# Giving out a load ring's slots by the program, and loading one weight matrix with one DMA, in a cached-attention decode kernel

## The chip, the core and the metric

The kernel runs on one core of one Trainium2 chip. The metric is device microseconds of one execution (us). Three runs of the kernel before gave 2533.29, 2533.44 and 2534.53 us; their median is 2533.44 us. One more execution was taken with the hardware profiler on: 2534.51 us.

## The reference: one decoding step of attention, mixed with a small feed-forward net

```
q = (x @ wq) as 32 heads of 128;   K, V caches: 32 heads x 65536 positions x 128, bf16
s = q . K * 128**-0.5;  p = softmax(s);  o = p @ V;   a = o @ wo
b = (silu(x @ w_gate) * (x @ w_up)) @ w_down          (512 -> 1792 -> 512)
g = sigmoid(sum(x * gate_w));   out = g * a + (1 - g) * b
```

x is one row of 512 numbers. The two caches are 512 MB each, together 1073.7 MB; w_gate, w_up and w_down have 1.835 MB each, wq and wo 4.19 MB each. Every byte of the caches is used once.

## The kernel before

**Tiles and steps.** Each head's cache is cut into G = 4 tiles of 16384 positions, so there are N = 128 K tiles and 128 V tiles, each of 4 MB: 128 partitions with 128 positions of 128 bf16 values, 32 KB in one piece per partition. The loop at line 355 goes through steps (n, v): K tile n and V tile v are loaded and worked on in one step. v trails n by 4, later by up to 8 (LAG, lines 344 to 352), and the last steps have a V tile alone.

**K tile n** (`products`, line 230; `scores`, line 249): VectorE multiplies the tile in place with the head's query (L240) and folds the 128 products of a position to 16 by three additions (L244). TensorE adds the last 16 with an identity matrix into the score bank S_ps (L254, 16 matmuls). After the fourth tile of a head, at the next step, come the maximum, the exponentials (L266 to L279) and, later, the sum.

**V tile v** (`values`, line 296): 32 matmuls (L302) with the exponentials as weights into O_ps. In one step TensorE runs values(v) first and scores(n) after it. After a head's last V tile the head is copied and turned to a column (L315, L323), and heads 0 to 15 are projected at once (`project`, L335); wo for heads 16 to 31 is loaded at the very end (`load_wo_end`, line 157) and these 16 heads are projected last.

**The ring.** All big loads (wq, K tiles, w_gate with w_up, w_down, V tiles, the last half of wo) go into one pool of SLOTS = 5 slots of 32 KB per partition (line 58, `big`, line 69). The pool hands a new tile the slot that its users gave back first. SyncE (SP) issues every load in the order of the program, and an issue waits until its slot's last users are done. In the trace, V tile 2 is issued at 107.05 us, when values(0) has ended, and K tile 7 at 111.39 us, when scores(4) has ended. The completions of all DMAs are counted on eight semaphores in turn, and an issue also waits for the DMA eight before it: the ninth DMA, first part of w_down, is issued at 8.41 us, when the first, x, has landed.

**The order at the start, on SP:** wq, K tile 0 in two halves, K tile 1, w_gate, w_up, gate_w (gwT, line 149), parts 0 and 1 of w_down (line 150), K tile 2, parts 2 to 7 of w_down (line 359), K tile 3, wo's first group (line 361), K tile 4, V tile 0, K tile 5, V tile 1 and so on. x itself (xT, line 76) comes over ScalarE's queue. w_down is laid out over 64 partitions, 28 KB each, and cut into eight DMAs of 8 partitions:

```
137	    HP = P // 2
138	    GT = F // HP
139	    wd_sb = wd_t[:HP, : GT * D].rearrange("p (t n) -> p t n", t=GT)
144	            lo = (0, 1, 2, 3, 32, 33, 34, 35)[i]
145	            part = slice(lo, lo + 29, 4)
146	            nc.sync.dma_start(out=wd_sb[part], in_=wd_rows[part])
```

**The feed-forward net** stands beside the first steps: `feed_forward_in` (line 169) after the products of step 1, `feed_forward_mid` (line 189) in step 2, ahead of the products. The mid part makes the hidden vector hT on VectorE, moves it from 128 to 64 partitions (two matmuls, L202, and a copy, L206), runs 28 matmuls with w_down (L209) and the gate's matmul (L213). `feed_forward_out` (line 218), after the products of step 3, scales the result and starts the output's accumulation with it (L226, L227).

**The end.** V tile 126 comes in two parts, tile 127 in five, and wo's last half in five (lines 365 to 367).

Of the kernel before, what the change touches and what calls it, by code (L numbers as in the profile page):

```python
# [8 lines left out]
ACT = mybir.ActivationFunctionType  # L9
ALU = mybir.AluOpType  # L10
AXIS = mybir.AxisListType
P = 128
# [3 lines left out]
NB = 128  # L16
SLOTS = 5
# [8 lines left out]
def kernel(  # L26
# [14 lines left out]
    nc = tc.nc  # L41
    bf16 = mybir.dt.bfloat16
    f32 = mybir.dt.float32

    _, H, Sk, Dh = A_k_cache.shape
    D = A_x.shape[2]
    F = B_w_gate.shape[1]
    KT = D // P
    FT = F // P
    G = Sk // (NB * P)  # L50
    NBH = Sk // P
    N = H * G
# [2 lines left out]
    scale = float(Dh) ** -0.5  # L55

    consts = ctx.enter_context(tc.tile_pool(name="consts", bufs=1))
    ring = ctx.enter_context(tc.tile_pool(name="ring", bufs=SLOTS))
    small = ctx.enter_context(tc.tile_pool(name="small", bufs=2))
    ppool = ctx.enter_context(tc.tile_pool(name="ppool", bufs=3))  # L60
    wo_pool = ctx.enter_context(tc.tile_pool(name="wo_pool", bufs=2))
# [3 lines left out]
    psum_m = ctx.enter_context(tc.tile_pool(name="psum_m", bufs=2, space=bass.MemoryType.PSUM))  # L65

    ctx.enter_context(tc.manual_schedule())

    def big(name):
        return ring.tile([P, NB * Dh], bf16, name=name, tag="big")  # L70


    xT = consts.tile([P, KT], bf16, name="xT")
    gwT = consts.tile([P, KT], bf16, name="gwT")
    with nc.allow_non_contiguous_dma(reason="small"):
        nc.scalar.dma_start(out=xT, in_=A_x[0, 0, :].rearrange("(p t) -> p t", t=KT))
    wq_t = big("wq_t")
    wq_sb = wq_t[:, : KT * H * Dh].rearrange("p (t f) -> p t f", t=KT)
    nc.sync.dma_start(out=wq_sb, in_=A_wq.rearrange("(p t) f -> p t f", t=KT))

    ident_f = consts.tile([P, P], f32, name="ident_f")
    make_identity(nc, ident_f[:])
    ident_b = consts.tile([P, P], bf16, name="ident_b")
# [15 lines left out]

    K_tiles, V_tiles, S_tiles, P_tiles, O_tiles = {}, {}, {}, {}, {}  # L100

    def load(dst, cache, n, name, cuts=(0, NB)):
        h, g = divmod(n, G)
        t = big(name)
        view = t.rearrange("p (j d) -> p j d", d=Dh)
        src = cache[0, h, g * NB * P : (g + 1) * NB * P, :].rearrange("(p j) d -> p j d", j=NB)
        for a, b in zip(cuts[:-1], cuts[1:]):
            nc.sync.dma_start(out=view[:, a:b, :], in_=src[:, a:b, :])
        dst[n] = view

    load(K_tiles, A_k_cache, 0, "K_t", (0, NB // 2, NB))
    load(K_tiles, A_k_cache, 1, "K_t")

    def queries(g):
        qg_ps = psum_m.tile([P, QG * Dh], f32, name="qg_ps", tag="misc")
# [13 lines left out]
        queries(g)  # L129


    gu_t = big("gu_t")
    wgu_sb = gu_t[:, : 2 * KT * F].rearrange("p (w t f) -> p w t f", w=2, t=KT)
    nc.sync.dma_start(out=wgu_sb[:, 0], in_=B_w_gate.rearrange("(p t) f -> p t f", t=KT))
    nc.sync.dma_start(out=wgu_sb[:, 1], in_=B_w_up.rearrange("(p t) f -> p t f", t=KT))
    wd_t = big("wd_t")
    HP = P // 2
    GT = F // HP
    wd_sb = wd_t[:HP, : GT * D].rearrange("p (t n) -> p t n", t=GT)
    wd_rows = B_w_down.rearrange("(p t) n -> p t n", t=GT)  # L140

    def load_wd(*which):
        for i in which:
            lo = (0, 1, 2, 3, 32, 33, 34, 35)[i]
            part = slice(lo, lo + 29, 4)
            nc.sync.dma_start(out=wd_sb[part], in_=wd_rows[part])

    with nc.allow_non_contiguous_dma(reason="small"):
        nc.sync.dma_start(out=gwT, in_=gate_w.rearrange("(p t) -> p t", t=KT))
    load_wd(0, 1)  # L150
    WG = 4
    wo_tiles = {}

    WH = H // 2
    wo_end = []

    def load_wo_end(cuts):
        t = big("wo_t")[:, : (H - WH) * D].rearrange("p (h n) -> p h n", n=D)
        rows = A_wo[WH * P :, :].rearrange("(h p) n -> p h n", p=P)
        for a, b in zip(cuts[:-1], cuts[1:]):  # L160
            nc.sync.dma_start(out=t[:, a:b, :], in_=rows[:, a:b, :])
        wo_end.append(t)

    def load_wo(g):
        wo_tiles[g] = wo_pool.tile([P, WG, D], bf16, name="wo_sb")
        rows = A_wo[g * WG * P : (g + 1) * WG * P, :]
        nc.sync.dma_start(out=wo_tiles[g], in_=rows.rearrange("(h p) n -> p h n", p=P))
# [21 lines left out]
    def feed_forward_mid(gu_sb, eg):  # L189
        nc.vector.tensor_scalar_add(eg, eg, 1.0)  # L190
        nc.vector.reciprocal(eg, eg)
        hprod = consts.tile([P, FT], f32, name="hprod")
        nc.vector.tensor_tensor(out=hprod, in0=gu_sb[:, :FT], in1=eg, op=ALU.mult)
        hT = consts.tile([P, FT], bf16, name="hT")
        nc.vector.tensor_tensor(out=hT, in0=hprod, in1=gu_sb[:, FT:], op=ALU.mult)
        xg = consts.tile([P, KT], f32, name="xg")
        nc.vector.tensor_tensor(out=xg, in0=xT, in1=gwT, op=ALU.mult)
        xs = consts.tile([P, 1], f32, name="xs")
        nc.vector.tensor_reduce(out=xs, in_=xg, axis=AXIS.X, op=ALU.add)
        h_ps = psum_m.tile([HP, GT], f32, name="h_ps", tag="misc")  # L200
        for r in range(2):
            nc.tensor.matmul(  # L202
                h_ps[:, r * FT : (r + 1) * FT], lhsT=ident_b[:, r::2], rhs=hT, start=True, stop=True
            )
        h2 = consts.tile([HP, GT], bf16, name="h2")
        nc.scalar.activation(out=h2, in_=h_ps, func=ACT.Copy)  # L206
        b_ps = psum_m.tile([1, D], f32, name="b_ps", tag="misc")
        for t in range(GT):
            nc.tensor.matmul(  # L209
                b_ps, lhsT=h2[:, t : t + 1], rhs=wd_sb[:, t, :], start=(t == 0), stop=(t == GT - 1)  # L210
            )
        g_ps = psum_m.tile([P, 1], f32, name="g_ps", tag="misc")
        nc.tensor.matmul(g_ps, lhsT=ones_f, rhs=xs, start=True, stop=True)  # L213
        eg2 = consts.tile([P, 1], f32, name="eg2")
        nc.scalar.activation(out=eg2, in_=g_ps, func=ACT.Exp, scale=-1.0)
        return b_ps, eg2

    def feed_forward_out(b_ps, eg2):

        nc.vector.tensor_scalar_add(eg2, eg2, 1.0)  # L220
        nc.vector.reciprocal(gval, eg2)
        rest = consts.tile([1, 1], f32, name="rest")
        nc.vector.tensor_scalar(
            out=rest, in0=gval[0:1, :], scalar1=-1.0, scalar2=1.0, op0=ALU.mult, op1=ALU.add
        )
        nc.scalar.activation(out=b_sb, in_=b_ps, func=ACT.Copy, scale=rest)  # L226
        nc.tensor.matmul(a_ps, lhsT=ones_f[0:1, 0:1], rhs=b_sb, start=True, stop=False)  # L227
# [117 lines left out]
    v = 0  # L345
# [8 lines left out]
    ff = done = tot_ps = None  # L354
    for n, v in steps:
        if n is not None and n > 1:
            load(K_tiles, A_k_cache, n, "K_t")
        if n == 2:
            load_wd(2, 3, 4, 5, 6, 7)
        if n == 3:  # L360
            load_wo(0)
        if v is not None:
            if v % (WG * G) == 2 * G and v // (WG * G) + 1 < WH // WG:
                load_wo(v // (WG * G) + 1)
            load(V_tiles, A_v_cache, v, "V_t", (0, NB) if v < N - 2 else (0, 64, NB) if v < N - 1 else (0, 32, 64, 96, 112, NB))
            if v == N - 1:
                load_wo_end((0, 4, 8, 12, 14, 16))
        if n == 2:
            ff = feed_forward_mid(*ff)
        halves = (0, NB // 2)  # L370
        vector = iter(()) if n is None else products(n)
        if n == 0:
            vector = (i for a in halves for i in products(n, a, a + NB // 2))
        top_of = None
        if n is None:
            top_of = H - 1 if S_tiles else None
        elif n % G == 0 and n > 0:
            top_of = n // G - 1
            vector = (i for a in halves for i in products(n, a, a + NB // 2))
        if top_of is not None:  # L380
            next(vector, None)
            mT_ps = row_max(top_of)
            next(vector, None)
            exponentials(top_of, mT_ps)
        for _ in vector:
            pass
        if n == 1:
            ff = feed_forward_in()
        if n == 3:
            feed_forward_out(*ff)  # L390
        if tot_ps is not None:
            weight(*tot_ps)
            tot_ps = None
        if done is not None:
            head_column(done, head_copy(done))
        if v is not None:
            values(v)
        if top_of is not None:
            tot_ps = top_of, total(top_of)
        if n is not None:  # L400
            scores(n)
        if done is not None and done < WH:
            project(done)
        done = v // G if v is not None and v % G == G - 1 else None
# [40 lines left out]
```

## Time and profile before

| What | Value |
|---|---|
| median of three runs | 2533.44 us |
| the profiled execution | 2534.51 us |
| its span, first to last instruction | 2532.6 us |
| read from HBM | 1087.64 MB, 429 GB/s over the span |
| VectorE (DVE) busy | 2175.5 us, 86% |
| TensorE (PE) busy | 1742.4 us, 69% |
| ScalarE (ACT) busy | 75.9 us, 3% |
| DMA queue q1 (SP's loads) | 42674 packets, 1087.66 MB, 99.7% of 16 engines' time |
| DMA queue q8 (instructions) | 53 packets, 0.87 MB, 0.1% |

The page cuts the span into 40 slices of 63.3 us and gives the DMA engines' share and rate in each. A load is cut into packets that 16 DMA engines move side by side; for each load the trace also holds the moment at which each of the engines that took part had counted its share as landed. "Spread" is used below for the time from the first of these counts to the last.

### The profile page before, as it was taken

The numbers are of one execution on the slowest core, as the hardware profiler recorded it, in microseconds if no ns is written. First come the engines' busy times: TensorE is split into PE (matmuls) and PEld (weight loads), VectorE is DVE, ScalarE is ACT, GpSimd is POOL, SyncE is SP. The second block draws the span as 40 slices with busy tenths as digits, with TensorE's granted clock in tenths as the row PEclk, the third lists the DMA queues.
The fourth block names the chain that finished last, engine by engine and source line by source line (L and its number), as shares of the span: only waits on it lengthen the run. The fifth ranks groups of instructions, "written<-read, shape, count | busy, mean of one in ns | idle before, by whom it ended". The sixth has DMA issues, their size and how long they took to land.

```text
span 2532.6 us, 15260 instructions
## 1 busy us (share of the span) xinstructions
PE 1742.4 (69%) x6738; PEld 712.1 (28%) x6738; DVE 2175.5 (86%) x784; ACT 75.9 (3%) x207; POOL 0.7 (0%) x6
## 2 busy tenths in 40 slices
PE   4677666776677666676776677667666776677679
PEld 2222222222222222222222223222222232222223
DVE  7998888888888999998888888888888888888860
ACT  1000000000000000000000000000000000000000
POOL 0000000000000000000000000000000000000000
PEclk7677777777777676677777777777777777777779
DMA  9999999999999999999999999999999999999998
GB/s 415 433 433 430 433 433 433 432 430 435 432 432 434 431 433 432 432 433 433 432 434 433 432 434 433 432 432 434 432 431 434 433 430 434 434 431 433 434 432 339
DMA packets 42884, 1088.63 MB, mean 430 GB/s; under 512 B 4737, under 2 KB 8834, under 8 KB 9090
## 3 DMA queue, kind: packets, MB, share of 16 engines
q1 hardware_dynamic: 42674, 1087.66, 99.7%
q8 instruction: 53, 0.87, 0.1%
q14 instruction: 13, 0.11, 0.0%
q10 hardware_dynamic: 144, 0.00, 0.0%
HBM read 1087.64 MB, written 0.00 MB: 429 GB/s over the span
## 4 chain that ended last, share of the span: by engine, by line
DMA 68%; PE 22%; DVE 10%; issue 1%; ACT 0%; DVEq 0%; SPq 0%
DMA V_t<-in_A_v_cache_dram 61%; PE O_ps L302 20%; DMA K_t<-in_A_k_cache_dram 5%; DVE K_t L240 5%; DVE K_t L244 5%; PE S_ps L254 1%; DMA wo_t<-in_A_wo_dram 1%; DMA wq_t<-in_A_wq_dram 0%; PE qg_ps L117 0%; DVE m L266 0%; PE oh_ps L323 0%; PE a_ps L335 0%; PE a_ps L227 0%; ACT P_sb L279 0%; DVE top L275 0%
## 5 line engine op out<-in xcount | busy, mean ns | idle before, releaser
L302 PE MATMUL O_ps<-V_t,P_sb 128*4 128x512 bf16 x4096 | 1157.3, 453 | 496.8 <-DMA V_t<-in_A_v_cache_dram 494.3
L240 DVE TENSOR_TENSOR K_t<-K_t,q_bc 128x16384 bf16<-128x16384 bf16 (+1 forms) x160 | 1117.2, 6983 | 254.4 <-DMA K_t<-in_A_k_cache_dram 232.9
L244 DVE TENSOR_TENSOR K_t<-K_t 128x4096 bf16<-128x4096 bf16 (+3 forms) x480 | 1030.9, 2148 | 14.3
L302 PEld LDWEIGHTS <-P_sb 128*4 128x4 bf16 x4096 | 393.9, 97 | 1241.0 <-issue 897.5
L254 PE MATMUL S_ps<-K_t,ident_b 128*128 128x128 bf16 x2048 | 466.0, 394 | 107.0 <-DVE K_t L244 106.9
L254 PEld LDWEIGHTS <-ident_b 128*128 128x128 bf16 x2048 | 227.6, 115 | 330.0 <-issue 140.2
L323 PE MATMUL oh_ps<-ident_f,O_sb 4*128 4x1 f32 x256 | 57.9, 343 | 74.1 <-ACT O_sb L315 74.1
L323 PEld LDWEIGHTS oh_ps<-ident_f,O_sb 4*128 4x128 f32 x256 | 55.2, 314 | 83.7 <-ACT O_sb L315 78.9
L270 PE MATMUL mT_ps<-diag,ones_f 128*128 128x128 f32 x64 | 23.6, 468 | 79.8 <-ACT diag L268 79.8
L268 ACT ACTIVATE diag<-ident_f,m 128x128 f32<-128x128 f32 x32 | 12.8, 401 | 2099.3 <-DVE m L266 2099.3
L317 DVE COPY O_sb<-O_ps 4x256 f32<-4x256 f32 x1 | 0.4, 414 | 52.1 <-ACT O_sb L315 52.1
L270 PEld LDWEIGHTS mT_ps<-diag,ones_f 128*128 128x128 f32 x64 | 14.7, 285 | 95.6 <-ACT diag L268 95.6
L266 DVE TENSOR_REDUCE m<-S_ps 128x1 f32<-128x512 f32 x32 | 21.9, 683 | 7.4 <-PE S_ps L254 7.4
L315 ACT ACTIVATE O_sb<-O_ps 4x512 f32<-4x512 f32 (+1 forms) x32 | 18.1, 566 | 131.0 <-PE O_ps L302 131.0
L279 ACT ACTIVATE P_sb<-S_ps,bias 128x512 bf16<-128x512 f32 x32 | 22.0, 687 | 1.0
L117 PE MATMUL qg_ps<-wq_t,X_bc 128*128 128x512 bf16 x32 | 8.6, 436 | 13.2 <-DMA wq_t<-in_A_wq_dram 13.2
L293 DVE RECIPROCAL recip<-tot_ps 128x1 f32<-128x1 f32 x32 | 5.1, 160 | 12.2 <-PE tot_ps L288 12.2
L209 PE MATMUL b_ps<-wd_t,h 64*1 64x512 bf16 x28 | 12.1, 629 | 4.3 <-DMA K_t<-in_A_k_cache_dram 4.3
L288 PEld LDWEIGHTS tot_ps<-rowsum,ones_f 128*128 128x128 f32 x64 | 9.5, 188 | 14.0 <-issue 14.0
L288 PE MATMUL tot_ps<-rowsum,ones_f 128*128 128x1 f32 x64 | 12.2, 260 | 0.0
L330 ACT ACTIVATE oT<-oh_ps,rg 128x1 bf16<-128x1 f32 x32 | 8.4, 263 | 76.6 <-PE oh_ps L323 76.6
L227 PE MATMUL a_ps<-b_sb,ones_f 1*1 1x512 f32 x2 | 1.9, 1032 | 12.1 <-ACT b_sb L226 12.1
(42 smaller groups left out, 73.8 us busy)
## 6 DMA issues: line engine op xcount, KB each, us to landing
K_t<-in_A_k_cache_dram SPq DMA_DIRECT2D x127, 4096.0 KB, 35.3
V_t<-in_A_v_cache_dram SPq DMA_DIRECT2D x126, 4096.0 KB, 29.1
wq_t<-in_A_wq_dram SPq DMA_DIRECT2D x1, 4096.0 KB
K_t<-in_A_k_cache_dram SPq DMA_DIRECT2D x2, 2048.0 KB, 16.8
V_t<-in_A_v_cache_dram SPq DMA_DIRECT2D x2, 2048.0 KB
V_t<-in_A_v_cache_dram SPq DMA_DIRECT2D x3, 1024.0 KB, 29.4
wo_sb<-in_A_wo_dram SPq DMA_DIRECT2D x4, 512.0 KB, 17.3
gu_t<-in_B_w_gate_dram SPq DMA_DIRECT2D x1, 1792.0 KB
```

Source lines behind the costliest of these rows:

```text
L209: nc.tensor.matmul(b_ps, lhsT=h2[:, t : t + 1], rhs=wd_sb[:, t, :], start=(t == 0), stop=(t == GT - 1))
L240: yield nc.vector.tensor_tensor(out=K, in0=K, in1=q_rep, op=ALU.mult)
L244: yield nc.vector.tensor_tensor(out=K[:, :, 0:half], in0=K[:, :, 0:half], in1=K[:, :, half : 2 * half], op=ALU.add,)
L254: nc.tensor.matmul(S_tiles[h][:, g * NB : (g + 1) * NB], lhsT=ident_b, rhs=K_tiles[n][:, :, c], start=(c == 0), stop=(c == WIDTH - 1),)
L266: nc.vector.tensor_reduce(out=m, in_=S_tiles[h], axis=AXIS.X, op=ALU.max)
L268: nc.scalar.activation(out=diag, in_=ident_f, func=ACT.Copy, scale=m)
L270: nc.tensor.matmul(mT_ps, lhsT=ones_f, rhs=diag, start=True, stop=True)
L279: nc.scalar.activation(out=P_tiles[h], in_=S_tiles[h], func=ACT.Exp, bias=bias, scale=scale, accum_out=rowsum[:, h : h + 1],)
L288: nc.tensor.matmul(tot_ps, lhsT=ones_f, rhs=rowsum[:, h : h + 1], start=True, stop=True)
L302: nc.tensor.matmul(O_tiles[h], lhsT=P_tiles[h][:, g * NB + j : g * NB + j + 4], rhs=V_tiles[n][:, j : j + 4, :], start=(g == 0 and j == 0) ...
L315: nc.scalar.activation(out=O_sb[:, :cut], in_=O_ps[:, :cut], func=ACT.Copy)
L323: nc.tensor.matmul(oh_ps, lhsT=O_sb[:, c * Dh : (c + 1) * Dh], rhs=ident_f[0:4, c : c + 1], start=(c == 0), stop=(c == 3),)
```

## The change

The pool of five slots becomes one tile `ring` of five slots' length, and `big` hands out its parts in strict rotation, the slot of five loads before; what a load waits for then follows from the part that it overwrites. w_down goes back to 128 partitions of 14 KB and is loaded by one DMA in step 3, behind K tile 3. x and gate_w change queues: gate_w goes over ScalarE's, x over SP's behind wq. wo's first group moves from step 3 to step 6. The mid part loses L202, L206 and its 28 matmuls; `feed_forward_out` runs 14 matmuls with w_down and moves ahead of the products of step 3. V tile 125 is loaded in two halves.

```diff
-    ring = ctx.enter_context(tc.tile_pool(name="ring", bufs=SLOTS))
+    ring = consts.tile([P, SLOTS * UNIT], bf16, name="ring")
+    taken = []
+    def big():
+        u = len(taken) % SLOTS
+        taken.append(u)
+        return ring[:, u * UNIT : (u + 1) * UNIT]
...
-        nc.scalar.dma_start(out=xT, in_=A_x[0, 0, :].rearrange("(p t) -> p t", t=KT))
+        nc.scalar.dma_start(out=gwT, in_=gate_w.rearrange("(p t) -> p t", t=KT))
...
     nc.sync.dma_start(out=wq_sb, in_=A_wq.rearrange("(p t) f -> p t f", t=KT))
+        nc.sync.dma_start(out=xT, in_=A_x[0, 0, :].rearrange("(p t) -> p t", t=KT))
...
-        nc.sync.dma_start(out=gwT, in_=gate_w.rearrange("(p t) -> p t", t=KT))
-    load_wd(0, 1)
+    wd_sb = wd_t[:, : FT * D].rearrange("p (t n) -> p t n", t=FT)
...
-        h_ps = psum_m.tile([HP, GT], f32, name="h_ps", tag="misc")
-        for r in range(2):
-            nc.tensor.matmul(
-                h_ps[:, r * FT : (r + 1) * FT], lhsT=ident_b[:, r::2], rhs=hT, start=True, stop=True
-            )
-        h2 = consts.tile([HP, GT], bf16, name="h2")
-        nc.scalar.activation(out=h2, in_=h_ps, func=ACT.Copy)
...
-        for t in range(GT):
-            nc.tensor.matmul(
-                b_ps, lhsT=h2[:, t : t + 1], rhs=wd_sb[:, t, :], start=(t == 0), stop=(t == GT - 1)
-            )
...
+    def feed_forward_out(hT, eg2):
+        b_ps = psum_m.tile([1, D], f32, name="b_ps", tag="misc")
+        for ft in range(FT):
+            nc.tensor.matmul(
+                b_ps,
+                lhsT=hT[:, ft : ft + 1],
+                rhs=wd_sb[:, ft, :],
+                start=(ft == 0),
+                stop=(ft == FT - 1),
+            )
...
-        if n == 2:
-            load_wd(2, 3, 4, 5, 6, 7)
         if n == 3:
+            nc.sync.dma_start(out=wd_sb, in_=B_w_down.rearrange("(p t) n -> p t n", t=FT))
+        if n == 6:
             load_wo(0)
...
-            load(V_tiles, A_v_cache, v, "V_t", (0, NB) if v < N - 2 else (0, 64, NB) if v < N - 1 else (0, 32, 64, 96, 112, NB))
+            load(V_tiles, A_v_cache, v, (0, NB) if v < N - 3 else (0, 64, NB) if v < N - 1 else (0, 32, 64, 96, 112, NB))
...
         if n == 2:
             ff = feed_forward_mid(*ff)
+        if n == 3:
+            feed_forward_out(*ff)
```

More of the change, by code (lines that the diff above doesn't have):

```diff
@@ L67 @@
     ctx.enter_context(tc.manual_schedule())
-    def big(name):
-        return ring.tile([P, NB * Dh], bf16, name=name, tag="big")
+    UNIT = NB * Dh
+    ring = consts.tile([P, SLOTS * UNIT], bf16, name="ring")
[4 more added lines that the diff above has]
+        return ring[:, u * UNIT : (u + 1) * UNIT]
     xT = consts.tile([P, KT], bf16, name="xT")
@@ L75 @@
     with nc.allow_non_contiguous_dma(reason="small"):
-        nc.scalar.dma_start(out=xT, in_=A_x[0, 0, :].rearrange("(p t) -> p t", t=KT))
-    wq_t = big("wq_t")
+        nc.scalar.dma_start(out=gwT, in_=gate_w.rearrange("(p t) -> p t", t=KT))
+    wq_t = big()
     wq_sb = wq_t[:, : KT * H * Dh].rearrange("p (t f) -> p t f", t=KT)
     nc.sync.dma_start(out=wq_sb, in_=A_wq.rearrange("(p t) f -> p t f", t=KT))
+    with nc.allow_non_contiguous_dma(reason="small"):
+        nc.sync.dma_start(out=xT, in_=A_x[0, 0, :].rearrange("(p t) -> p t", t=KT))
     ident_f = consts.tile([P, P], f32, name="ident_f")
@@ L100, with load @@
     K_tiles, V_tiles, S_tiles, P_tiles, O_tiles = {}, {}, {}, {}, {}
-    def load(dst, cache, n, name, cuts=(0, NB)):
+    def load(dst, cache, n, cuts=(0, NB)):
         h, g = divmod(n, G)
-        t = big(name)
+        t = big()
         view = t.rearrange("p (j d) -> p j d", d=Dh)
@@ L109, in load @@
         dst[n] = view
-    load(K_tiles, A_k_cache, 0, "K_t", (0, NB // 2, NB))
-    load(K_tiles, A_k_cache, 1, "K_t")
+    load(K_tiles, A_k_cache, 0, (0, NB // 2, NB))
+    load(K_tiles, A_k_cache, 1)
     def queries(g):
@@ L129 @@
         queries(g)
-    gu_t = big("gu_t")
+    gu_t = big()
     wgu_sb = gu_t[:, : 2 * KT * F].rearrange("p (w t f) -> p w t f", w=2, t=KT)
@@ L135 @@
     nc.sync.dma_start(out=wgu_sb[:, 1], in_=B_w_up.rearrange("(p t) f -> p t f", t=KT))
[L136 to L148, printed above, removed]
-        nc.sync.dma_start(out=gwT, in_=gate_w.rearrange("(p t) -> p t", t=KT))
-    load_wd(0, 1)
+    wd_t = big()
+    wd_sb = wd_t[:, : FT * D].rearrange("p (t n) -> p t n", t=FT)
     WG = 4
@@ L157, in load_wo_end @@
     def load_wo_end(cuts):
-        t = big("wo_t")[:, : (H - WH) * D].rearrange("p (h n) -> p h n", n=D)
+        t = big()[:, : (H - WH) * D].rearrange("p (h n) -> p h n", n=D)
         rows = A_wo[WH * P :, :].rearrange("(h p) n -> p h n", p=P)
@@ L199, in feed_forward_mid @@
         nc.vector.tensor_reduce(out=xs, in_=xg, axis=AXIS.X, op=ALU.add)
-        h_ps = psum_m.tile([HP, GT], f32, name="h_ps", tag="misc")
-        for r in range(2):
-            nc.tensor.matmul(
-                h_ps[:, r * FT : (r + 1) * FT], lhsT=ident_b[:, r::2], rhs=hT, start=True, stop=True
-            )
-        h2 = consts.tile([HP, GT], bf16, name="h2")
-        nc.scalar.activation(out=h2, in_=h_ps, func=ACT.Copy)
-        b_ps = psum_m.tile([1, D], f32, name="b_ps", tag="misc")
-        for t in range(GT):
-            nc.tensor.matmul(
-                b_ps, lhsT=h2[:, t : t + 1], rhs=wd_sb[:, t, :], start=(t == 0), stop=(t == GT - 1)
-            )
         g_ps = psum_m.tile([P, 1], f32, name="g_ps", tag="misc")
@@ L215, in feed_forward_mid @@
         nc.scalar.activation(out=eg2, in_=g_ps, func=ACT.Exp, scale=-1.0)
-        return b_ps, eg2
-    def feed_forward_out(b_ps, eg2):
+        return hT, eg2
+    def feed_forward_out(hT, eg2):
[8 more added lines that the diff above has]
+            )
         nc.vector.tensor_scalar_add(eg2, eg2, 1.0)
@@ L356 @@
         if n is not None and n > 1:
-            load(K_tiles, A_k_cache, n, "K_t")
-        if n == 2:
-            load_wd(2, 3, 4, 5, 6, 7)
+            load(K_tiles, A_k_cache, n)
         if n == 3:
+            nc.sync.dma_start(out=wd_sb, in_=B_w_down.rearrange("(p t) n -> p t n", t=FT))
+        if n == 6:
             load_wo(0)
@@ L388 @@
             ff = feed_forward_in()
-        if n == 3:
-            feed_forward_out(*ff)
         if tot_ps is not None:
```

## The prediction

> **What bounds the kernel now.** I read the page's strips first, then the table of stages, the chain at the end, and last the landing counts of single loads. On the page:
>
> ```profile
> PE 1742.4 (69%) x6738; PEld 712.1 (28%) x6738; DVE 2175.5 (86%) x784; ACT 75.9 (3%) x207; POOL 0.7 (0%) x6
> ...
> DMA  9999999999999999999999999999999999999998
> ...
> q1 hardware_dynamic: 42674, 1087.66, 99.7%
> q8 instruction: 53, 0.87, 0.1%
> ...
> DMA 68%; PE 22%; DVE 10%; issue 1%; ACT 0%; DVEq 0%; SPq 0%
> ```
>
> No compute engine is full; the DMA engines are, in every slice but the last. Two answers of the table of stages (us, busy of each engine, clock, DMA share, GB/s), one of the middle, one of the end, show where they are not:
>
> ```profile
> 1000.00:1500.00 500.00, 347.82 (x1319) 141.50 (x1320) 453.64 (x163) 14.19 (x40) 0.00 (x0) 0.74 1.00 433
> ```
> ```profile
> 2505.00:2510.00 5.00, 5.00 (x25) 1.99 (x24) 0.00 (x0) 0.00 (x0) 0.00 (x0) 1.00 0.95 401
> 2510.00:2515.00 5.00, 5.00 (x25) 1.99 (x24) 0.00 (x0) 0.00 (x0) 0.00 (x0) 1.00 0.91 365
> 2515.00:2520.00 5.00, 5.00 (x25) 1.97 (x24) 0.00 (x0) 0.00 (x0) 0.00 (x0) 1.00 0.79 287
> 2520.00:2525.00 5.00, 5.00 (x24) 1.87 (x22) 0.00 (x0) 0.00 (x0) 0.00 (x0) 1.00 0.54 148
> ```
>
> The share fades over 20 us instead of falling at once: some of the 16 DMA engines are done early and others late. The chain's last pieces name who waits for the late ones:
>
> ```profile
> 2472.70 31.39 DMA V_t<-in_A_v_cache_dram
> ...
> 2504.16 20.87 DMA wo_t<-in_A_wo_dram
> 2525.03 0.04 issue
> 2525.07 1.02 PE a_ps L335 x4
> 2526.09 0.98 PE oh_ps L323 x8
> 2527.07 2.69 PE a_ps L335 x12
> ```
>
> So the end is set by the DMA engine that lands its share last, plus 7.5 us (2525.07 to 2532.6). The fifth part of wo lands at 2529.11 and its first matmul starts at 2529.16, so even these 7.5 us hang on that engine.
>
> The landing counts tell when it falls behind. Up to w_up the 16 engines count within 0.74 us. After w_down's parts they stand in two halves, and they stay so (us after the first count, sorted):
>
> ```
> K tile 3 (first 60.10):   0 0 0 .1 .3 .3 .4 .4 | 8.3 8.4 8.4 8.4 8.5 8.7 8.8 9.9
> V 127, last part (2507.04): 0 0 6.8 6.8 6.9 7.1 7.4 7.8 8.3 8.4 8.5 8.6 9.1 12.7 15.5 16.6
> ```
>
> Each part of w_down shows one count about 1.1 us after its issue and eight later ones, and has 8 packets of 28 KB: all eight parts used the same eight engines (call them A; the others B), 8.35 us of work that B did not have. The rest of the spread grows slowly, as instruction packets (q8, 53 of 16 KB, 0.93 us each) fall on some engines: by following the steps of the sorted counts, some six of B and two or three of A. An A engine with both, 8.35 + 8.25 us, is the late one at 16.6.
>
> **The change, part by part.**
>
> *w_down in one DMA of 128 partitions.* Its shape is that of w_gate and w_up (128 packets of 14336 B, 8 on each of 16 engines). Between w_gate's and w_up's counts lie 40.49 - 36.17 = 4.32 us. So each engine gets 4.32 us where A had 8.35 and B nothing. The late A engine comes to 16.6 - 8.35 + 4.32 = 12.6; the latest of B, at 8.5 now, to 8.5 + 4.32 = 12.8. The later of the two counts: the end moves from 16.6 to 12.8, **-3.8 us**. The range of this term: if the instruction packets lie otherwise, one step of a sorted count is 1.2 to 1.4 us, so -2.5 to -5.2.
>
> *V tile 125 in halves.* K tile 0 in halves took (22.24 - 17.36) x 2 = 9.76 us where tile 1 whole took 31.92 - 22.24 = 9.68: **+0.1 us** on every engine. In return TensorE, idle for 1.62 us before tile 125 and then busy for 20.88 us up to 2525.02, starts up to 1.62 us earlier. Without that it would nearly follow the DMA anyway; with it, the last four matmuls on V tile 127 wait for its last part (2523.67 before). Both ends of the chain, wo's first part and TensorE, then move with the late DMA engine, so I take nothing more.
>
> *x behind wq.* x lands with wq (13.2 instead of 8.4), the four copies X_bc (0.63 us together) then come ahead of the queries, which start at about 13.7 instead of 13.23. K tile 0's first half lands at 18.05 and the first query group took 2.5 us (13.23 to 15.73), so 16.2 is early enough: 0. K tile 2's issue moves from 21.86 to 22.4, with loads queued to 41: 0.
>
> *Feed-forward.* TensorE loses 2 + 28 matmuls and gains 14: 12.10 us / 28 = 0.432, so 6.0 us instead of 12.4. It is not on the path, and neither are the small VectorE operations, which move from behind step 3's products to ahead of them. But K tile 5 takes w_down's slot and now waits for the 14 matmuls behind scores(2): VectorE's chain comes 0.8 us earlier (K tile 2 no longer behind two parts of w_down), scores(2) ends near 73.6, the matmuls at 79.7 (72.48 before). Behind K5 on SP stand V1, K6 and all later loads. The DMA engines run dry when V tile 0 is in: its first count 80.83 + 4.32 - 1.36 (wo's first group now comes later) = 83.8. An issue took 1.2 us to its first packet at the start (0.74 to 1.95): 80.9, 2.9 us to spare. Cost 0; without the cover a microsecond for each microsecond late.
>
> *Strict rotation.* Within a step the pool gave the next V load the slot of values (two steps back), the next K load that of scores. Rotation gives V the slot of K tile n-2, free after scores(n-2), some 3.65 us later (16 matmuls L254), and K the older slot of a V tile, but behind V on SP. So V issues come about 3.7 us later, K issues about the same. A steady V load was issued some 29 us ahead of its last landing, of which its own 9.68 us is transfer; 25 us is left, 15 us of queue in front of it. The thinnest place is V tile 2: issued after scores(4), 110.6, first packet 111.8; K tile 6 and wo's group are in at 109.89 + 4.32 = 114.2. 2.4 us to spare: 0. The later waits of wo's parts are for landings of V parts, which come earlier with the late engine. Bounds for all these holds together: 0 and, with both thin places missed by as much as they have to spare, 5 us.
>
> *Fewer DMAs.* Seven landing packets less on each A engine, 9 ns each: in the 4.32 already.
>
> Sum: -3.8 + 0.1 = **-3.7 us**. On the profiled execution 2534.51 gives 2530.8; its median runs are 1.07 us below it, so 2533.44 gives **2529.7 us**, -0.15%. About 0.2% (5.1 us) is what a measurement of this kernel can tell from no change, so this counts as the same, on the fast side.
>
> **A rule against it.** A late engine only matters if each engine has a rate of its own. In the last slices, when three engines are left, an 8 KB packet takes 0.309 us, as with 16 at work; 32 KB packets take 1.213 us at the median and at the 99th percentile. The Trainium skill's page "DMA: Bandwidth & Descriptors" (Where 436 GB/s comes from) says that a transfer from HBM is bound on the HBM side, at about 358 GB/s per core; by that the bytes alone would count, sharing them out otherwise would give 0, and the time would stay at 2533.4. This trace disagrees: 433 GB/s for 500 us on end.
>
> **Rivals.**
> 1. *The spread is there, but evening it out gives nothing:* the shared rate binds, or the instruction packets fall on other engines, so that another one is as late as now. For it: where those packets fall is read off sorted counts, not seen. Against: the packet times above and the halves after w_down. 0 + 0.1 gives 2533.5. Chance 0.14.
> 2. *More than counted:* the late engine has one instruction packet less (1.2 to 1.4 us) and TensorE's earlier start helps the last heads: -3.7 - 1.3 - 0.4 gives 2528.0, just past -0.2%. Chance 0.10.
> 3. *Slower: w_down's slot is given back late.* If the 14 matmuls run behind scores(3) instead of ahead of it (86.6 + 3.65 = 90.3, then 6.0: 96.3), K tile 5's first packet comes at 97.5, 13.7 us after the queue is empty: 2529.7 + 13.7 = 2543.4. It decides from 82.6 us on (83.8 - 1.2); from 91.4 on the total is slower by over 0.2%. For it: these matmuls now wait on one DMA queued behind K tile 3. Against: that DMA lands near 65, and TensorE's order has the matmuls ahead of scores(3). Chance 0.08.
> 4. *One tile, false waits:* if a load waited for the last use of any part of the ring, load and work would take turns: 9.7 + 16.7 (VectorE on one K tile) us or more per step instead of 19.4 per pair, +7 x 128, beyond 3400. Against: q_bc is one tile written in eight parts, and the first product starts at 18.15, when five of the eight copies are still to come. Chance 0.03.
>
> **Numbers.** Forecast 0.65. Faster by over 0.2%: rival 2 and a little of the forecast's tail, 0.12. Slower by over 0.2%: rivals 3 and 4, 0.11. Within: 0.77. The range, 2527.2 to 2534.0, takes in -2.5 to -5.2 of the first term, rival 1 and most of rival 2, and leaves out rivals 3 and 4.
>
> **What would show it.** K tile 3's counts within 2.5 us instead of 9.9; the spread of the last V part near 8.5 instead of 16.6; the four last windows of the table fuller, and shorter by some 4 us; DMA share 1.00 between 75 and 120; SP's V issues together with K issues. It would be wrong if a gap stands in DMA around 84 or 114, if the late engine is still 16 us behind, or if TensorE ends later than the last landing of wo.

## The result and the profile after

| Kernel | Median, us (range, runs) | Profiled execution | Its span |
|---|---|---|---|
| before, run beside it | 2534.61 (2533.07 to 2537.65, 8) | | |
| after | 2540.56 (2540.39 to 2540.95, 8) | 2540.47 | 2538.7 |

The ratio after / before is 1.0023 [1.0014, 1.0032]: the change makes the kernel about 6 us slower. The forecast was 2529.7 us and the range ended at 2534.0, so time and sign were both missed. On the profiled executions the forecast was 2534.51 - 3.7 = 2530.8; the miss is 2540.47 - 2530.8 = 9.7 us. This number is what the experiments have to explain.

The page of after, the lines that answer to those shown of before:

```profile
PE 1734.0 (68%) x6722; PEld 710.7 (28%) x6722; DVE 2175.6 (86%) x784; ACT 75.7 (3%) x206; POOL 0.7 (0%) x6
...
DMA  9999999999999999999999999999999999999998
GB/s 414 432 429 429 433 432 431 430 430 430 431 433 431 429 431 432 431 432 430 430 432 433 430 431 431 433 431 430 432 431 432 430 431 431 432 432 431 430 433 357
...
q1 hardware_dynamic: 42834, 1087.66, 99.8%
q8 instruction: 52, 0.85, 0.1%
...
DMA 58%; PE 27%; DVE 14%; issue 1%; ACT 0%; SPq 0%; DVEq 0%
```

The DMA engines are still full in every slice but the last, and q1 fills 99.8% of their time (99.7% before). No wait has opened a gap. In the table of stages (us, busy of PE, PEld, DVE, ACT, POOL, clock, DMA share, GB/s) the stretch that the prediction named, the middle and the end give:

```profile
75.00:120.00 45.00, 29.37 (x113) 11.32 (x112) 44.69 (x17) 2.06 (x5) 0.00 (x0) 0.75 1.00 427
1000.00:1500.00 500.00, 347.86 (x1309) 140.79 (x1310) 451.52 (x162) 14.20 (x40) 0.00 (x0) 0.74 1.00 431
2510.00:2515.00 5.00, 5.00 (x25) 1.99 (x24) 0.00 (x0) 0.00 (x0) 0.00 (x0) 1.00 1.00 421
2515.00:2520.00 5.00, 3.88 (x19) 1.46 (x18) 0.00 (x0) 0.00 (x0) 0.00 (x0) 1.00 0.96 392
2520.00:2525.00 5.00, 5.00 (x24) 1.95 (x23) 0.00 (x0) 0.00 (x0) 0.00 (x0) 1.00 0.75 303
2525.00:2530.00 5.00, 4.71 (x23) 1.78 (x21) 0.00 (x0) 0.00 (x0) 0.00 (x0) 1.00 0.76 283
```

The share falls off late and over a shorter stretch, as it should with a smaller spread. The row of the middle is the one that tells where the time went: share 1.00 as before, but 431 GB/s where before had 433. Engines that never pause move fewer bytes. A gap or a late issue would lower the share; here the share stays and the rate falls, so each packet takes longer. The lengths of the packets of the loads, from the trace, by size:

| Packet | before, mean ns | after, mean ns |
|---|---|---|
| 32 KB (2032 on each engine in before, 2024 in after) | 1214.4 | 1218.2 |
| 8 KB | 309.0 | 312.6 |
| 4 KB | 159.0 | 160.6 |
| instructions, 16 KB (q8) | 929 | 1067 |

Of the 32 KB packets, the 1st and the 99th percentile of before are both 1213 ns; in after the quartiles are 1214, 1216 and 1220, and one packet in five still takes 1213.

The end of the chain of waits (start, us, what) has the same pieces as before, 6.2 us later:

```profile
2478.59 31.42 DMA ring<-in_A_v_cache_dram
...
2510.08 21.11 DMA ring<-in_A_wo_dram
...
2531.23 1.02 PE a_ps L326 x4
...
```

And the issues on SP (start, us, line), where the prediction had its thin places:

```profile
39.19 0.33 SPq L115 DMA_DIRECT2D ring<-in_A_k_cache_dram  x1
39.57 0.42 SPq L350 DMA_DIRECT2D ring<-in_B_w_down_dram  x1
...
78.38 0.33 SPq L115 DMA_DIRECT2D ring<-in_A_k_cache_dram  x1
78.76 0.42 SPq L115 DMA_DIRECT2D ring<-in_A_v_cache_dram  x1
...
108.98 0.33 SPq L115 DMA_DIRECT2D ring<-in_A_v_cache_dram  x1
109.36 0.42 SPq L115 DMA_DIRECT2D ring<-in_A_k_cache_dram  x1
```

K tile 5 is issued at 78.38 (79.7 was expected), V tile 2 at 108.98 (110.6 was expected): both in time. The landing counts (us after the first, sorted) show the part of the forecast that did come true:

```
after, K tile 3 (first 60.14):          0 0 .1 .1 .1 .1 .2 .2 .2 .3 .3 .3 .4 .4 .5 1.7
after, V 127, last part (first 2518.33): 0 .2 .3 .7 .9 2.0 3.4 7.5 9.6 9.8 9.8 9.9 11.1 11.2 11.3 11.4
```

The two halves behind w_down are gone (spread 1.71 instead of 9.87), and the last spread is 11.4 instead of 16.6. The late engine is less late against the first one; the whole stream has become slower. In this text the last spread is that of V tile 127's last part.

### The profile page after: what moved, and what is told of

Read it like the earlier page. It is cut to its first block, busy times and chain, and to the rows that moved or that the text cites. A ratio compares the mean times of both kernels' runs of the same rounds, so it can differ in the third digit from the quotient of the medians.

```text
span 2538.7 us, 15127 instructions
## 1 busy us (share of the span) xinstructions
PE 1734.0 (68%) x6722; PEld 710.7 (28%) x6722; DVE 2175.6 (86%) x784; ACT 75.7 (3%) x206; POOL 0.7 (0%) x6
## 3 DMA queue, kind: packets, MB, share of 16 engines
q1 hardware_dynamic: 42834, 1087.66, 99.8%
## 4 chain that ended last, share of the span: by engine, by line
DMA 58%; PE 27%; DVE 14%; issue 1%; ACT 0%; SPq 0%; DVEq 0%
DMA ring<-in_A_v_cache_dram 53%; PE O_ps L293 19%; PE S_ps L245 8%; DVE ring L231 7%; DVE ring L235 6%; DMA ring<-in_A_k_cache_dram 5%; DMA ring<-in_A_wo_dram 1%; DVE m L257 0%; PE oh_ps L314 0%; PE a_ps L326 0%; ACT P_sb L270 0%; DVE top L266 0%; SPq L115 0%; ACT O_sb L306 0%; DVE out_sb L404 0%
## 5 line engine op out<-in xcount | busy, mean ns | idle before, releaser
L293 PE MATMUL O_ps<-ring,P_sb 128*4 128x512 bf16 x4096 | 1155.6, 452 | 515.3 <-DMA ring<-in_A_v_cache_dram 512.6
L231 DVE TENSOR_TENSOR ring<-ring,q_bc 128x16384 bf16<-128x16384 bf16 (+1 forms) x160 | 1117.3, 6983 | 256.9 <-DMA ring<-in_A_k_cache_dram 256.9
L235 DVE TENSOR_TENSOR ring<-ring 128x4096 bf16<-128x4096 bf16 (+3 forms) x480 | 1031.1, 2148 | 14.3
L245 PE MATMUL S_ps<-ring,ident_b 128*128 128x128 bf16 x2048 | 465.7, 394 | 120.4 <-DVE ring L235 120.3
L259 ACT ACTIVATE diag<-ident_f,m 128x128 f32<-128x128 f32 x32 | 12.8, 401 | 2114.7 <-DVE m L257 2114.7
L124 PE MATMUL qg_ps<-ring,X_bc 128*128 128x512 bf16 x32 | 9.7, 479 | 13.5 <-DVE X_bc L98 13.5
L279 PE MATMUL tot_ps<-rowsum,ones_f 128*128 128x1 f32 x64 | 12.2, 260 | 0.0
L98 DVE COPY X_bc<-xT 128x128 bf16<-128x128 bf16 x4 | 0.6, 222 | 12.2 <-DMA xT<-in_A_x_dram 12.2
L266 DVE TENSOR_REDUCE top<-mT_ps 128x1 f32<-128x128 f32 x32 | 9.1, 284 | 1.0 <-PE mT_ps L261 1.0
```

Of the source, the lines that this page charges most:

```text
L124: nc.tensor.matmul(qg_ps, lhsT=X_bc[:, t, :], rhs=wq_sb[:, t, g * QG * Dh : (g + 1) * QG * Dh], start=(t == 0), stop=(t == KT - 1),)
L231: yield nc.vector.tensor_tensor(out=K, in0=K, in1=q_rep, op=ALU.mult)
L235: yield nc.vector.tensor_tensor(out=K[:, :, 0:half], in0=K[:, :, 0:half], in1=K[:, :, half : 2 * half], op=ALU.add,)
L245: nc.tensor.matmul(S_tiles[h][:, g * NB : (g + 1) * NB], lhsT=ident_b, rhs=K_tiles[n][:, :, c], start=(c == 0), stop=(c == WIDTH - 1),)
L259: nc.scalar.activation(out=diag, in_=ident_f, func=ACT.Copy, scale=m)
L279: nc.tensor.matmul(tot_ps, lhsT=ones_f, rhs=rowsum[:, h : h + 1], start=True, stop=True)
```

## The experiments

**The theories.** What can make full DMA engines take 0.3% longer for each packet, from one end of the run to the other? *Place:* the five slots moved in SBUF. The built programs list the first byte of each tile in its partition. In before the five slots begin at byte 30976 and every 32768 from there; 30976 is 121 x 256. In after the one tile `ring` begins at 16512, which is 128 past a multiple of 256. If rows that don't begin at a multiple of 256 bytes cost more, the loads pay on each packet. *Order (rival):* rotation changes which slot is loaded while which is read, so loads meet the engines' accesses differently. *Queue (rival):* one of the other parts (x, w_down as one DMA, tile 125) does it. *Step (rival):* the halves that w_down's parts had made kept the engines apart, and engines in step slow each other's packets. The texts written ahead of the runs call place theory A and step theory L; their other letters are explained where they stand. The first series (experiments 1 to 4) makes one part of the change at a time; the second (6 to 9) and the third (5, 10, 11) move nothing but the place, except for 5, which is one more part. All of these kernels compute the whole reference. The kernel before was run beside each series (medians 2534.57, 2534.68 and 2534.44 us), and ratios are to that.

**1. After once more, unedited** (`a1_after_again`).

> The changed kernel once more, unedited. In its first trace every 32 KB packet takes about 1218 ns on average where before has 1213 (4.6 ns, 0.33%, from 33.8 us on), and the spread of the last V part is 11.4 us instead of 16.6. Theory K (the slower packets belong to the kernel): again 1218 ns and about 2540.5 us. Theory C (they belong to the state of the chip at that run): 1213 ns in some run of it, and then about 2540.5 - 8.3 = 2532 us or less.

Measured: 2540.57 us (2540.2 to 2540.82, 10 runs), 1.0024 [1.0014, 1.0033]; 32 KB packets 1218.2 ns at the mean, last spread 11.8. The result stands, and so do the longer packets.

**2. The ring alone** (`e1_ring`): before, with slots given out by the program.

```diff
-    ring = ctx.enter_context(tc.tile_pool(name="ring", bufs=SLOTS))
+    UNIT = NB * Dh
+    ring = consts.tile([P, SLOTS * UNIT], bf16, name="ring")
...
-        return ring.tile([P, NB * Dh], bf16, name=name, tag="big")
+        u = len(taken) % SLOTS
+        taken.append(u)
+        return ring[:, u * UNIT : (u + 1) * UNIT]
```

> Before, with only the ring given out by the program in strict rotation. Theory R (the ring's place or its waits slow the packets): packets near 1218 ns from the start of the run on, +8 us, 2541 to 2543. Theory S (order or layout at the start slows them): packets 1213 ns, spread 16.6, time as before within 1 us, since no DMA engine ran empty.

Measured: 2562.97 us (4 runs), 1.0111 [1.0094, 1.0128]. The ring begins at 16512; 32 KB packets 1218.6 ns. Most of the loss is another thing, and it stands at the start. On the page of this kernel:

```profile
DMA  7899999999999999999999999999999999999998
GB/s 327 365 429 429 434 431 431 432 430 432 432 431 431 431 432 431 432 430 432 431 433 429 433 431 431 431 433 430 433 431 430 432 430 433 431 433 428 432 432 357
```

Its issues on SP, and its longest waits there (line, waited for, us in total, times, longest) up to 110 us:

```profile
41.13 1.46 SPq L151 DMA_DIRECT2D ring<-in_B_w_down_dram  x2
46.37 0.34 SPq L113 DMA_DIRECT2D ring<-in_A_k_cache_dram  x1
66.78 3.99 SPq L151 DMA_DIRECT2D ring<-in_B_w_down_dram  x6
76.14 0.33 SPq L113 DMA_DIRECT2D ring<-in_A_k_cache_dram  x1
```
```profile
SPq L151 <- DMA ring<-in_B_w_gate_dram: 32.4, 1, 32.4
SPq L113 <- DVE ring L249: 16.9, 2, 12.6
SPq L151 <- DMA ring<-in_A_k_cache_dram: 12.8, 1, 12.8
...
SPq L151 <- DMA ring<-in_B_w_up_dram: 4.3, 1, 4.3
```

w_down's parts go to the fifth slot, which no load had used. Yet the first is issued only at 41.13 us, just after w_up has landed in the fourth slot; before had issued it at 8.41. In one tile, these parts wait for loads into other slots. This is the prediction's rival 4, but only for the parts with every fourth partition: the loads of after, which take whole runs of partitions, are issued without such a wait. That the stride over partitions is the reason is inferred from these kernels alone. Between 40 and 77 us the DMA engines idle 341 us, summed over 16, 21 us each; in before they are never idle there.

**3. w_down alone as one DMA** (`e2_wd_one`): before, with w_down in the 128 rows of after, issued where parts 0 and 1 were, and 14 matmuls in place of 2 + 28.

```diff
-    load_wd(0, 1)
+    nc.sync.dma_start(out=wd_sb, in_=B_w_down.rearrange("(p t) n -> p t n", t=FT))
...
-        h2 = consts.tile([HP, GT], bf16, name="h2")
...
-        if n == 2:
-            load_wd(2, 3, 4, 5, 6, 7)
```

> Before, with only w_down as one DMA on 128 partitions (in the place of its parts 0 and 1) and the 14 matmuls in place of 30. If evening out the engines is worth what was predicted and nothing else follows: spread about 12, -3.8 us, 2529.7. Theory L (engines that run in step slow each other's packets, and the halves that w_down's parts made had kept them apart): packets 1218 ns and +8.3 - 3.8, about 2538. Theory R: packets 1213 ns.

Measured: 2540.87 us (9 runs), 1.0028 [1.0018, 1.0037]; last spread 10.9, 32 KB packets 1218.1 ns. The spread falls as forecast, and still the kernel is slower, without any ring. The pool's slots moved here too: the small tile h2 is gone, and the slots begin at 30912, 192 past a multiple of 256. So *order* is not needed for the loss.

**4. x and gate_w alone** (`e3_x_swap`): the two queues exchanged, as in after.

```diff
-        nc.scalar.dma_start(out=xT, in_=A_x[0, 0, :].rearrange("(p t) -> p t", t=KT))
+        nc.scalar.dma_start(out=gwT, in_=gate_w.rearrange("(p t) -> p t", t=KT))
...
+        nc.sync.dma_start(out=xT, in_=A_x[0, 0, :].rearrange("(p t) -> p t", t=KT))
```

> Before, with only x and gate_w changing queues (x behind wq on SP). The first loads' counts then spread over 0.47 us instead of 0.74, as in the changed kernel. Theory P (this first offset between the engines decides how their packets meet for the whole run): 1218 ns and +8 us. Otherwise 1213 ns and the time as before within 0.5 us.

Measured: 2534.61 us (10 runs), 0.9998 [0.9989, 1.0008]; slots at 30976, 32 KB packets 1214.4 ns at the mean, as in before. Nothing.

**5. V tile 125 alone in halves** (`e4_v125`, of the third series).

```diff
-(0, NB) if v < N - 2 else (0, 64, NB) if v < N - 1
+(0, NB) if v < N - 3 else (0, 64, NB) if v < N - 1
```

> Before, with only V tile 125 in two halves. The prediction's term is +0.1 us for eight more packets per engine; TensorE's earlier start gives nothing, since the last DMA engine sets the end: 2534.7, within 0.5 us of before. No tile moves in SBUF, so packets 1213 ns.

Measured: 2534.39 us (10 runs), 1.0000 [0.9990, 1.0009]; 32 KB packets 1214.4 ns. Nothing.

**6. Only the place moved: before, 64 bytes further** (`f1_before_off64`). A tile of 64 bytes per partition that nothing reads is put ahead of the small tiles; the slots begin at 31040.

```diff
+    pad = consts.tile([P, 32], bf16, name="pad")
+    nc.gpsimd.memset(pad, 0.0)
```

> Before, with one unused tile of 64 B per partition ahead of the others, which moves the ring's slots from byte 30976 of the partition (121 x 256) to 31040 (64 past a multiple of 256). Nothing else moves. Theory A (where a row begins in the partition decides the packets' time: every load whose rows do not begin at a multiple of 256 B costs each packet some 4.6 ns): 1218 ns from about 30 us on, +8.3 us, 2542 to 2543. Theory L (engines in step slow each other; w_down's halves keep them apart): 1213 ns, spread 16.6, 2534.6.

Measured: 2545.04 us (5 runs), 1.0038 [1.0024, 1.0053]: 10.4 us slower, with 32 KB packets of 1218.3 ns and a last spread of 16.4, that of before. The middle of this kernel:

```profile
1000.00:1500.00 500.00, 344.19 (x1316) 140.72 (x1315) 451.69 (x162) 14.19 (x40) 0.00 (x0) 0.75 1.00 431
```

The share of 1.00 and the 431 GB/s are those of after, from a program whose loads, order and queues are those of before. The halves behind w_down are there too (K tile 3's counts spread over 10.0 us), so neither *order* nor *queue* nor *step* is needed for the loss. This run decides for *place*.

**7. Only the place moved: after, brought back to a multiple of 256** (`f2_after_on256`). 128 unused bytes ahead of the ring; it begins at 16640 = 65 x 256.

```diff
     UNIT = NB * Dh
+    pad = consts.tile([P, 64], bf16, name="pad")
+    nc.gpsimd.memset(pad, 0.0)
     ring = consts.tile([P, SLOTS * UNIT], bf16, name="ring")
```

> The changed kernel with 128 unused bytes ahead of its ring, which so begins at byte 16640 (65 x 256) instead of 16512 (128 past a multiple). Theory A: packets 1213 ns throughout, the spread near 11, 2540.6 - 8.3 = 2532.3, or, if the prediction's other terms hold in full, 2534.6 - 3.7 = 2530.9. Theory L: still 1218 ns and 2540.6.

Measured: 2530.63 us (2530.5 to 2530.82, 10 runs), 0.9983 [0.9973, 0.9992]: 4.05 us faster than before, 9.9 faster than after. 32 KB packets 1214.2 ns at the mean, last spread 10.3. The middle and four late stages, and the end of the chain:

```profile
1000.00:1500.00 500.00, 347.50 (x1332) 141.36 (x1331) 450.96 (x161) 13.06 (x38) 0.00 (x0) 0.76 1.00 433
...
2505.00:2510.00 5.00, 5.00 (x25) 1.97 (x24) 0.00 (x0) 0.00 (x0) 0.00 (x0) 1.00 0.98 413
2510.00:2515.00 5.00, 5.00 (x25) 1.99 (x24) 0.00 (x0) 0.00 (x0) 0.00 (x0) 1.00 0.85 331
2515.00:2520.00 5.00, 4.73 (x23) 1.82 (x22) 0.00 (x0) 0.00 (x0) 0.00 (x0) 1.00 0.75 272
2520.00:2525.00 5.00, 4.73 (x26) 2.22 (x24) 0.41 (x1) 0.64 (x2) 0.00 (x0) 1.00 0.61 213
```
```profile
2500.51 20.88 DMA ring<-in_A_wo_dram
...
2521.42 1.02 PE a_ps L328 x4
```

433 GB/s is back, with the engines in step (K tile 3's counts within 1.67 us), and the first matmul of the end starts at 2521.42 instead of 2525.07, 3.65 us earlier.

**8. w_down alone, at a multiple of 256** (`f3_wd_one_on256`): experiment 3 with 64 unused bytes; slots at 30976 again.

> The kernel with w_down alone as one DMA (2540.9 with its slots at 192 past a multiple of 256), with 64 unused bytes, so that the slots stand at 30976 as in before. Theory A: 1213 ns, spread 11 to 13, and the even w_down alone shows its worth: -3.8 by the prediction, 2530.8. Theory L: 1218 ns, 2540.9.

Measured: 2530.51 us (2530.37 to 2531.05, 10 runs), 0.9983 [0.9974, 0.9993]; 1214.2 ns, last spread 10.2. One DMA for w_down, with a spacer, gives all that the aligned after gives; the ring, the queues of x and gate_w and tile 125 add nothing measurable. Its chain ends on TensorE:

```profile
2469.72 30.69 DMA V_t<-in_A_v_cache_dram
...
2500.45 20.88 PE O_ps L288 x96
2521.32 0.86 PE a_ps L321 x4
```

Without tile 125 in halves TensorE has become the last to end, as the prediction had said ("nearly follow the DMA anyway"), at the same moment as the DMA in f2.

**9. The ring alone, at a multiple of 256** (`f4_ring_on256`): experiment 2 with 128 unused bytes ahead of the ring.

> The kernel with only the ring given out by the program (2563.0; ring at 16512), with 128 unused bytes ahead of the ring (16640). Its loads of w_down's parts on strided partitions waited for loads into other slots and left the DMA engines empty between 40 and 77 us, 353 engine-us or 22 us. Theory A: packets 1213 ns and 8 us less, about 2555; the gaps at the start stay. If the rotation itself cost time, gaps would stand later in the run too.

Measured: 2554.07 us (4 runs), 1.0074 [1.0059, 1.0089]; most 32 KB packets 1213 ns. 8.9 us of experiment 2's loss is place; the other 19.4 us stays with the waits of w_down's parts: the engines idle 335 us between 40 and 77 us, 21 each, and less than 1 us in any hundred from 100 to 2500. The gaps also let the engines draw level, although w_down still goes to eight of them: K tile 3's counts lie within 0.65 us instead of 9.87, and the last spread is 10.4 instead of 16.6, which gives part of the 21 back. So the start accounts for the 19.4 us, and no cost of rotation shows behind it.

**10. After, with the small tiles moved and the ring not** (`g1_after_rest_moved`): the 128 unused bytes stand behind the ring.

```diff
     ring = consts.tile([P, SLOTS * UNIT], bf16, name="ring")
+    pad = consts.tile([P, 64], bf16, name="pad")
+    nc.gpsimd.memset(pad, 0.0)
```

> The changed kernel with the 128 unused bytes behind its ring instead of ahead of it: the ring stays at 16512 (128 past a multiple of 256), all other tiles move as they did when the ring moved. Theory A, for the loads' own rows: 1218 ns and 2540.6 as before the move. If it was the place of the other tiles (VectorE's and TensorE's operands) that mattered: 1213 ns and 2530.6.

Measured: 2540.67 us (9 runs), 1.0025 [1.0015, 1.0035], 431 GB/s in the middle:

```profile
1000.00:1500.00 500.00, 345.51 (x1309) 139.86 (x1310) 451.49 (x163) 14.20 (x40) 0.00 (x0) 0.75 1.00 431
```

In the built programs of 7 and 10 every other tile of the loop has the same place (x at 180480, wo's groups at 203328 and 207424); the ring alone begins at 16640 in one and at 16512 in the other, and 10.0 us lie between them. It is the place of the ring, not that of the tiles behind it, nor the extra tile.

**11. Before, 32 bytes further** (`g2_before_off32`): as 6, with 16 columns; slots at 31008.

> Before, with 32 unused bytes ahead of the other tiles, slots at 31008, 32 past a multiple of 256. Theory A with any remainder alike (64, 128 and 192 cost 10.4, 9.9 and 10.4 us): 2545. If only the part of 256 B that is missing counts, a remainder of 32 would cost another sum than 64.

Measured: 2546.63 us (4 runs), 1.0049 [1.0034, 1.0064]: 12.2 us slower, 32 KB packets 1219.3 ns. Of the four shifts that were run, the smallest costs the most.

All places together; the two kernels of a pair differ in the place alone:

| Slots begin, bytes past a multiple of 256 | Mean 32 KB packet, ns | Against the same kernel at a multiple, us |
|---|---|---|
| 0 (before, x, V 125, and 7, 8) | 1214.2 to 1214.4 | |
| 0 (9, with its gaps at the start) | 1214.9 | |
| 32 (11 against before) | 1219.3 | +12.2 |
| 64 (6 against before) | 1218.3 | +10.4 |
| 128 (1 against 7) | 1218.2 | +9.9 |
| 128 (2 against 9) | 1218.6 | +8.9 |
| 192 (3 against 8) | 1218.1 | +10.4 |

## Why the prediction was wrong, point by point

**The failed step** is the one called *Strict rotation*. It treats the ring becoming one tile as a new order of slots and new waits, and costs it at 0 with an upper bound of 5 us for late issues. On order and waits it was right (experiment 9; V tile 2 at 108.98). That the edit also moves the slots in SBUF is nowhere in the working. The move to 128 bytes past a multiple of 256 made each 32 KB packet 4.0 ns longer (1218.2 against 1214.2 in f2): 2024 packets on an engine give 8.1 us, and the smaller packets 0.4 us more between them. That is by how much the first engine is later: V tile 127's last part is first counted at 2518.33 instead of 2509.76, 8.57 us. The last spread adds 1.15 us (11.43 against 10.28). Together 9.7 of the 9.81 us between the profiled executions of f2 and after. The longer instruction packets (1067 ns instead of 932) would fit the 1.15 us, but which engines they fall on is not shown, and after once more had a spread of 11.8. The same step failed in *Feed-forward* without being seen: dropping the 56-byte tile h2 alone moves the pool's slots off the boundary (experiment 3).

**w_down in one DMA, -3.8:** right. f3, which has this part and the boundary, is 4.17 us faster than before, f2 4.05, and on the profiled executions the end's first matmul moves by 3.65. The last landing of V 127 was put at 2507.04 + 12.8 + 0.1 = 2519.9; in f2 it is at 2509.76 + 10.28 = 2520.04. That w_down's load on eight engines made the late one late is thus shown. The way the engines were told apart is not: by the prediction's terms the first count would come at 2507.04 + 4.32 + 0.1 = 2511.5 and the spread would be near 8.5, and f2 has 2509.76 and 10.3. Both misses lie with the first engine and not with the last landing, which alone sets the time; on which engine each instruction packet falls stays open.

**V tile 125, x behind wq:** 0 measured for both (5 and 4), as forecast.

**Feed-forward's wait:** K tile 5 came 1.3 us earlier than forecast, and the 14 matmuls took 4.9 us instead of 6.0; no gap.

**The rule against it:** by the shared rate, evening out the engines would have given 0. Both f2 and f3 gained, with the same bytes to load, so each engine's own load does set the end here.

**Rivals:** none of the four was the case. Rivals 1 (0.1 us slower) and 2 (5.4 us faster) concern the term of w_down; with the ring on the boundary the change gains 4.05 us, next to the forecast's 3.7. Rival 4's mechanism exists (experiment 2), but not in this change. What was missing is a rival for the layout: the prediction asked of each edit what it does in time, and of none what it does to addresses.

**What would show it:** K tile 3's counts (within 1.71), the DMA share of 1.00 between 75 and 120 and the issues came as named. The last spread shrank, but to 11.4 (10.3 in f2) and not to 8.5; the late windows came some 6 us late instead of early. None of the signs named there for a wrong forecast appeared. The one that did, 431 against 433 GB/s at share 1.00, was not on the list.

## What to carry to other kernels

Where full DMA engines set the time, an edit that adds, drops or moves any tile, one of 56 bytes too, can move the destinations of all loads: look up where they begin, and keep them on multiples of 256 bytes, with a spacer if need be; here 64 or 128 bytes of spacer gave 10 us back. In a profile, read rate and share together: the same share at a lower rate means longer packets, and a search among waits does not find them. And count bytes by engine: w_down's DMAs over 8 partitions loaded eight engines, and the full stream of before carried that to its end; only the gaps of experiments 2 and 9 evened it out.

## What the runs showed of the hardware

- **The place of a load's rows in SBUF.** At 32, 64, 128 and 192 bytes past a multiple of 256 a 32 KB packet takes 4 to 5 ns longer than at a multiple (1218.1 to 1219.3 against 1214.2 to 1214.4), 0.3 to 0.4%. Both places on a multiple, 30976 and 16640, are odd multiples of 256; an even one was not run. The excess does not follow the bytes: with 32 bytes past, packets of 4, 8 and 32 KB are longer by 2.9, 5.5 and 4.9 ns. The Trainium skill's page "DMA: Bandwidth & Descriptors" (How a descriptor splits into AXI transactions) says that a transaction must start at a multiple of 256 B, and that a descriptor which starts elsewhere begins with one from the boundary below, whose unused bytes still cost beats. That agrees with the boundary found here. Its beats don't order these costs: as an estimate from its rule, a 32 KB descriptor gets 1, 2, 4 and 6 beats more at 32, 64, 128 and 192 past, where the runs show +4.9, +3.9, +4.0 and +3.9 ns; one transaction more, 129 instead of 128, is the same for all four. The page speaks of reads; these are writes into SBUF, so the mechanism stays argued, the price is shown. VectorE and TensorE work on the same shifted rows, and no run here moves a load's rows without them.
- **It begins late.** In after the first longer packets are at 33.8 us, in 1, 3 and 6 between 29.8 and 33.8; in after the packets of wq and of K tiles 0 and 1 are as long as in before, though they go into the same ring and VectorE is at work on K tile 0 from 18.08 us on. In e1, behind the gaps between 40 and 77 us, most packets are short again up to 150 us, and from 150 to 200 us the median is 3 ns longer. What starts and stops the excess, no run here tests.
- **Instruction packets pay too.** The 16 KB packets of q8 took 929 ns in before, 932 in f2 and 1067 in after, though the slots are not their destination. That is 15% where the loads' packets have 0.3%; why it is so much, no run here shows.
- **A lasting skew.** 8.35 us of work given to eight of sixteen engines at 10 to 70 us still delays the late engine at 2500 us: with 4.32 us on each engine instead (f2), the last landing is 3.6 us earlier (2520.04 against 2523.67). Even so the spread of f2 grows from 1.7 us at K tile 3 to 10.3 at the end. That instruction packets, about one in 48 us, do this is read off the steps of the counts, not shown.
